# Token tiles turned by transposing DMAs instead of TensorE in an attention, FFN and MoE kernel

## The chip, the cores and the metric

The kernel runs on one core of a Trainium2 chip. The metric is the device time of one execution in microseconds (us). Engines are called PE (TensorE; PEld is its weight load), DVE (VectorE), ACT (ScalarE), POOL (GpSimd) and SP (SyncE, which only issues DMAs here).

## The reference

Three stages follow each other; the output of each is the input of the next, and all of it is float32.

```python
# attention: q, k, v are (2, 8, 768, 64); 8 global keys, window of 96
scores = np.where(keep, scale * q @ k.T + bias, -1e9)
out = softmax(scores) @ v                      # x: (1536, 512)
# gated FFN, 512 -> 1536 -> 512
xn = x / sqrt(mean(x * x) + 1e-6) * rms_g
x = (silu(xn @ w_gate) * (xn @ w_val)) @ w_out
# top-2 of 8 experts, each 512 -> 1024 -> 512
noisy = x @ w_gate2 + log1p(exp(x @ w_noise)) * noise
top2, top2_w = ...                             # softmax over the two
for e in range(8):
    for k in range(2):
        mask = top2[:, k] == e
        out[mask] += top2_w[mask, k, None] * (np.maximum(x[mask] @ w1[e], 0) @ w2[e])
```

## The kernel before

The 1,536 tokens stand in 12 tiles of 128 rows. Products that need float32 accuracy are run as three products of a high and a low part (`xTh`/`xTl`, `gh`/`gl` and `zh`/`zl` for activations, `sa` and `sb` for the two weight matrices of an expert): ACT writes the high part by a copy that rounds, and DVE or POOL subtracts it from the source for the low part.

The FFN is visited by groups of tiles and pieces of its hidden width (`VISITS`). When the last piece of a group of tiles is done (`finish`), the tiles' outputs `x` are written to the DRAM tensor `x2d` and the group is routed: `route(g)` turns each tile of 128 tokens x 512 features into 4 blocks of 128 features x 128 tokens (four 128x128 transposes `pr` on PE into PSUM, L777, then one copy `x2T` on ACT, L782), multiplies them with the gate weights (`lg`, L784), picks two experts, counts ranks (`sel`, L811 to L814) and scatters the tokens' numbers and gains into the DRAM table `metad`. There are five groups (4, 2, 2, 2 and 2 tiles). After the third, the most used expert of the first 8 tiles is read into a register (`lead`), and its first 256 rows become unit 0.

The experts run as nine units. Unit 0 and unit 1 are the early and the late 256 rows of the leading expert, units 2 to 8 the other seven experts with at most 480, 448, 424, 408, 392, 384 and 368 rows. A unit's life is: SP fetches its slots `me` from `metad` (L918), POOL gathers its token rows from `x2d` in tiles of 128 (`xg`, L939), PE turns each by four transposes (`pg`, L949), and ACT and DVE write `gh` and `gl` from PSUM (L953, L954). Then for eight pieces f of the hidden width come `up` (`pz`, L982; 12 products), ReLU (`zh` on ACT, `zl` on DVE) and `down` (12 products). Gathering and turning for a unit happen during the unit ahead of it. Weights come in as `wab` by SP, two DMAs per f.

`down` has two forms. In units 2 to 6 ("wide": L1022) the result `ac` has features on the partitions and tokens along the row, so it is copied to SBUF (`oT`, two 128xcap copies on ACT, L1049, and two on DVE, L1047), turned on PE by four transposes per tile of 128 tokens (`pb`, L1054), and only then multiplied by its gain and added to the old output rows (`y`, DVE, L1060), which POOL scatters to the output (L1065). In the other units the result comes out by tokens.

The order of instructions on each engine comes from a scheduler that simulates the program, with a few forced orders (`follow`). Every engine runs its list strictly in order, so an instruction that waits holds up all that stand behind it.

Of the kernel before, what the change touches and what calls it, by code (L numbers as in the profile page):

```python
# [19 lines left out]
P = 128  # L20
# [85 lines left out]
def fused(ctx: ExitStack, tc: tile.TileContext, q, k, v, n_global, n_local, w_gate, w_val, w_out,  # L106
# [98 lines left out]
    x2d = dr.tile([NT, DM], F32, name="x2d")  # L205
    metad = dr.tile([E * CAP, 2], I32, name="metad")
# [498 lines left out]
    def down(ci, t0, nt, f, d):  # L705
# [62 lines left out]
    def route(g):  # L768
# [3 lines left out]
        for t in range(GT):  # L772
            ti = G0[g] + t
            pt = ps.tile([P, 512], F32, name=f"pr{ti}", tag=("t", "t2", "s")[t % 3])
            p3 = pt.rearrange("p (a b) -> p a b", a=DC)
            for c in range(DC):
                nc.tensor.transpose(p3[:, c, :], x2t[ti][:, c * P:(c + 1) * P], ident)  # L777
            xt = sb.tile([P, DC, P], F32, name=f"x2T{ti}", tag="n2", bufs=N2)
            if last and t % 2:
                nc.vector.tensor_copy(xt, p3)  # L780
            else:
                nc.scalar.activation(xt, p3, AF.Copy)  # L782
# [124 lines left out]
    class Unit:  # L907
        def __init__(self, n, wkey, e, s0, cap):
# [3 lines left out]
            self.rows = G0[LEAD + 1] * P if n == 0 else NT  # L912

# [22 lines left out]
        def gather(self, s):  # L936
            m = self.tiles[s][1]
            xg = sb.tile([P, DM], F32, name=f"xg{self.n}_{s}", tag="n2", bufs=N2)
            self.last = nc.gpsimd.indirect_dma_start(  # L939
                out=xg[:m], out_offset=None, in_=x2d[:self.rows], in_offset=bass.IndirectOffsetOnAxis(ap=self.ic[:m, s:s + 1], axis=0))  # L940
            self.xg[s] = xg

        def turn(self, s, behind=None):
            m = self.tiles[s][1]
            xg = self.xg.pop(s)
            pt = ps.tile([P, 512], F32, name=f"pg{self.n}_{s}", tag="to"[s % 2])
# [5 lines left out]
            ss = slice(s * P, s * P + m)  # L952
# [10 lines left out]
        def run(self, side):  # L963
# [78 lines left out]
            if wide:  # L1042
                oT = [pools["b"].tile([P, 2, 512], F32, name=f"oT{n}_{x}", tag="raw", bufs=NRAW["b"]) for x in range(2)]
                for c in range(DC):
                    o = oT[c // 2][:, c % 2, :cap]
                    if c % 2:
                        nc.vector.tensor_copy(o, acc[c][:, :cap])  # L1047
                    else:
                        nc.scalar.activation(o, acc[c][:, :cap], AF.Copy)  # L1049
# [240 lines left out]
```

## Time and profile before

| | |
|---|---|
| median of 3 runs | 796.21 us (795.85 to 796.44) |
| profiled execution | 792.5 us, span 790.8 us, granted clock 0.991 |
| PE busy | 765.7 us (97%) |
| DVE busy | 469.0 us (59%) |
| ACT busy | 358.1 us (45%) |
| POOL busy | 308.4 us (39%) |

The span reaches from the first to the last instruction. Busy time is the time in which an engine executes something; a PE that is busy through a whole stretch sets the pace of that stretch, and other engines matter there only where they make PE wait.

### The profile page before, as it was taken

Reading aid. Unit: us, or ns where it says so; the run is one execution under the profiler, and the core shown is the slowest. Engines: PE = TensorE matmul, PEld = TensorE weight load, DVE = VectorE, ACT = ScalarE, POOL = GpSimd, SP = SyncE. Lnnn points to the kernel's source line nnn. Section 1 sums busy time; section 2 is a strip of 40 time slices with the busy share of each in tenths; the row PEclk is TensorE's granted clock in tenths of the full one; section 3 lists DMA queues with packets and bytes.
Section 4 is the critical chain, followed back from the end, with each engine's and each line's share of the span. In section 5 each row is a group of like instructions: output and inputs, shape, how many; then the busy total and the mean of one; then the engine's idle time right before and its main releaser. Section 6 shows DMA issues by size and latency. Waiting matters only on the chain. (4 is left out here: it accounts for less than half of the span.)

```text
span 790.8 us, 13766 instructions
## 1 busy us (share of the span) xinstructions
PE 765.7 (97%) x5019; PEld 692.0 (88%) x5019; DVE 469.0 (59%) x1081; ACT 358.1 (45%) x792; POOL 308.4 (39%) x343
## 2 busy tenths in 40 slices
PE   9899999999999999999999999899999999999993
PEld 6788999999788888889999888788999999999993
DVE  7988776766487888334454577433534454545542
ACT  6777566656444343123333465433343434344440
POOL 3457742331385576002431253531524343424311
PEclk9999999999999999999999999999999999999998
DMA  8654442250242430011109229953545638362011
GB/s 193 149 158 108 112 110 48 52 163 2 83 131 86 127 107 1 1 54 28 26 3 231 64 40 280 281 168 123 173 135 170 199 109 258 109 221 76 36 40 36
DMA packets 116839, 88.77 MB, mean 112 GB/s; under 512 B 49449, under 2 KB 100649, under 8 KB 116768
## 3 DMA queue, kind: packets, MB, share of 16 engines
q1 hardware_dynamic: 107920, 65.43, 30.2%
q0 software_dynamic: 7120, 19.27, 7.2%
q10 hardware_dynamic: 1728, 3.15, 1.3%
q8 instruction: 41, 0.67, 0.4%
q14 instruction: 30, 0.25, 0.1%
HBM read 75.18 MB, written 13.34 MB: 112 GB/s over the span
## 5 line engine op out<-in xcount | busy, mean ns | idle before, releaser
L982 PE MATMUL pz<-gh,sa 128*128 128x256 f32 (+7 forms) x576 | 156.8, 340 | 0.0
L982 PEld LDWEIGHTS pz<-gh,sa 128*128 128x128 f32 x576 | 104.0, 189 | 4.7
L982 PE MATMUL pz<-gl,sa 128*128 128x256 f32 (+7 forms) x288 | 97.6, 339 | 0.0
L715 PE MATMUL acc<-wo,dh 128*128 128x512 f32 x288 | 89.0, 400 | 1.0 <-ACT dh L701 1.0
L1022 PE MATMUL ac<-zh,sb 128*128 128x480 f32 (+4 forms) x320 | 86.3, 364 | 0.0
L989 ACT ACTIVATE zh<-pz 128x256 fp32r<-128x256 f32 (+7 forms) x72 | 35.1, 487 | 108.8 <-PE pz L982 106.4
L990 DVE SCALAR_TENSOR_TENSOR zl<-pz,zh 128x256 fp32r<-128x256 f32 (+7 forms) x72 | 39.8, 553 | 72.6 <-ACT zh L989 72.3
L688 PE MATMUL pz<-xTh,wg 128*128 128x256 f32 x352 | 75.0, 289 | 2.4 <-ACT wg L641 1.3
L688 PE MATMUL pz<-xTh,wv 128*128 128x256 f32 x352 | 75.3, 290 | 0.0
L670 ACT ACTIVATE sa<-wab 128x512 fp32r<-128x512 f32 x72 | 45.3, 631 | 56.6 <-PE ac L1022 39.6
L688 PEld LDWEIGHTS pz<-xTh,wg 128*128 128x128 f32 x352 | 58.9, 192 | 4.8 <-ACT wg L641 1.5
L674 DVE TENSOR_TENSOR sa<-wab,sa 128x512 fp32r<-128x512 f32 x51 | 36.4, 715 | 41.7 <-ACT sa L670 41.3
L1022 PEld LDWEIGHTS ac<-zh,sb 128*128 128x128 f32 x320 | 58.0, 188 | 3.2
L702 POOL TENSOR_TENSOR dl<-u,dh 128x256 fp32r<-128x256 f32 (+1 forms) x38 | 38.7, 1019 | 56.7 <-ACT dh L701 41.7
L715 PEld LDWEIGHTS acc<-wo,dh 128*128 128x128 f32 x288 | 51.3, 189 | 9.9 <-ACT dh L701 1.7
L688 PEld LDWEIGHTS pz<-xTh,wv 128*128 128x128 f32 x352 | 58.9, 193 | 0.3
L939 POOL DMA_INDIRECT xg<-x2d,ic x30 | 30.8, 1027 | 69.9 <-PE pg L949 63.1
L982 PEld LDWEIGHTS pz<-gl,sa 128*128 128x128 f32 x288 | 54.6, 190 | 2.4
L429 ACT ACTIVATE p<-s,mx 128x256 f32<-128x256 f32 (+1 forms) x96 | 46.2, 483 | 21.8 <-DVE mx L426 21.6
L892 POOL DMA_INDIRECT metad<-meta,si x24 | 23.8, 991 | 82.4 <-DVE si L864 76.3
L715 PE MATMUL acc<-wo,dl 128*128 128x512 f32 x144 | 53.0, 400 | 0.2 <-POOL dl L702 0.2
L1022 PE MATMUL ac<-zl,sb 128*128 128x480 f32 (+4 forms) x160 | 53.0, 358 | 0.0
(249 smaller groups left out, 1856.4 us busy)
## 6 DMA issues: line engine op xcount, KB each, us to landing
wab<-in_moe_w_dram SPq DMA_DIRECT2D x128, 256.0 KB, 5.0
rg<-in_moe_w_gate_dram SPq DMA_DIRECT2D x12, 512.0 KB, 4.1
rv<-in_moe_w_val_dram SPq DMA_DIRECT2D x12, 512.0 KB, 3.7
ro<-in_moe_w_out_dram SPq DMA_DIRECT2D x12, 512.0 KB, 3.5
vn<-in_v_dram SPq DMA_DIRECT2D x12, 256.0 KB, 4.1
out_dram<-zero SPq DMA_DIRECT2D x1, 3072.0 KB, 13.2
x2d<-x ACTq DMA_DIRECT2D x12, 256.0 KB, 5.1
kn<-in_k_dram SPq DMA_DIRECT2D x11, 256.0 KB, 3.2
```

What stands on the lines that cost most here:

```text
L429: state["e"] = nc.scalar.activation(p[:, :W], s[:, :W], AF.Exp, scale=-1.0, bias=mx[:, h:h + 1], accum_out=sm[:, h:h + 1]).ins
L670: cp = nc.scalar.activation(wp[:, 0], src, AF.Copy)
L674: (nc.gpsimd if pool else nc.vector).tensor_sub(wp[:, 1], src, wp[:, 0].bitcast(F32))
L688: mm = nc.tensor.matmul(pz, a[:, cs], x[:, tt:tt + nt, c, :], start=(n == 0), stop=(n == 3 * DC - 1))
L702: (nc.gpsimd if ci < len(CHUNKS) - 1 else nc.vector).tensor_sub(dl, u, dh.bitcast(F32))
L715: nc.tensor.matmul(acc[t], a[:, tt], w, start=(f == CHUNKS[ci][0] and n == 0), stop=(end and n == 2))
L892: st = nc.gpsimd.indirect_dma_start(out=metad, out_offset=bass.IndirectOffsetOnAxis(ap=si[:, t, kk:kk + 1], axis=0), in_=meta[:, G0[g] + t ...
L939: self.last = nc.gpsimd.indirect_dma_start(out=xg[:m], out_offset=None, in_=x2d[:self.rows], in_offset=bass.IndirectOffsetOnAxis(ap=self.i ...
L982: mm = nc.tensor.matmul(pz[:, :cap], a[:, cs], x[:, c, :cap], start=(k == 0), stop=(k == 3 * DC - 1))
L989: nc.scalar.activation(dh[:, :cap], pz[:, :cap], AF.Relu)
L990: nc.vector.scalar_tensor_tensor(dl[:, :cap], pz[:, :cap], 0.0, dh[:, :cap].bitcast(F32), op0=ALU.max, op1=ALU.subtract)
L1022: nc.tensor.matmul(acc[c][:, :cap], w[:, c * P:(c + 1) * P], a[:, :cap], start=(f == 0 and k == 0), stop=(f == FB2 - 1 and k == 2))
```

## The change

A float32 row of 512 numbers is stored as 1,024 halves of 16 bits, first the 512 low halves and then the 512 high halves. A DMA that transposes 16-bit elements turns the 128 x 1,024 matrix into 8 blocks of 128 x 128, and one ACT copy puts low and high halves together again as float32 (1,024 elements per partition).

- POOL splits each of the 12 tiles into halves (`halve`, a copy of 1,024 16-bit elements), and SP writes them to a new DRAM tensor `x2p`, beside `x2d`, which stays.
- Routing turns 10 of the 12 tiles by this DMA (`turned`); the last group's two still go by PE.
- Units 0 and 3 to 8 gather from `x2p` and turn by DMA, 24 tiles in all. Units 1 and 2 are as before.
- The five wide units copy each `ac` out of PSUM as halves, in three pieces where one was, turn 4 tiles each by DMA, 20 in all, and merge them on ACT. DVE reads the merged `pb` from SBUF.

This takes 216 of the 128x128 transposes off PE, and the ten routing copies off ACT. It adds 54 transposing DMAs and 12 writes on SP's queue, 54 merging copies on ACT, and 12 copies and 5 small memsets on POOL.

```diff
+    def turned(words, m, src, name, shape, tag, bufs):
+        nc.sync.dma_start_transpose(words[:, :, :m], src)
+        xt = sb.tile(shape, F32, name=name, tag=tag, bufs=bufs)
+        x3 = xt.rearrange("p (c q) -> p c q", c=DC) if len(shape) == 2 else xt
+        x4 = x3[:, :, :m].bitcast(U16).rearrange("p c (q t) -> p t c q", t=2)
+        nc.scalar.activation(x4, words[:, :, :m].rearrange("p (t c) q -> p t c q", t=2), AF.Copy)
+        return x3
...
+    def halve(ti, behind=None):
+        hw = split2[ti] = sb.tile([P, 2, 2 * DM], U16, name=f"hw{ti}", tag="words", bufs=2)
+        cp = nc.gpsimd.tensor_copy(hw[:, 0].rearrange("p (t n) -> p t n", t=2), x2t[ti].bitcast(U16).rearrange("p (n t) -> p t n", t=2))
...
+        nc.sync.dma_start(x2p[ti * P:(ti + 1) * P, :], hw[:, 0])
...
+            if not last:
+                hw = split2[ti]
+                xt = turned(hw[:, 1].rearrange("p (a b) -> p a b", a=2 * DC), P, hw[:, 0], f"x2T{ti}", [P, DC, P], "n2", N2)
...
+            self.halved = n == 0 or n > 2
...
+            if self.halved:
+                m2 = -(-m // 16) * 16
+                if s % 2 == 0:
+                    self.hw = sb.tile([P, 2, 2 * DC, P], U16, name=f"hg{self.n}_{s}", tag="words", bufs=2)
+                x3 = turned(self.hw[:, s % 2], m2, xg[:m2], f"xc{self.n}_{s}", [P, 512], "wc", 2)[:, :, :m]
+                nc.scalar.activation(self.gh[:, :, ss], x3, AF.Copy)
+                nc.vector.tensor_sub(self.gl[:, :, ss], x3, self.gh[:, :, ss].bitcast(F32))
+                return
...
                 for c in range(DC):
...
+                    for x in range(2):
+                        w = min(2 * P, cap - 2 * x * P)
+                        src = acc[c][:, 2 * x * P:2 * x * P + w].bitcast(U16)
...
+                        for s0, k, q in pieces:
...
+                            if c % 2:
+                                nc.vector.tensor_copy(o, i)
+                            else:
+                                nc.scalar.activation(o, i, AF.Copy)
...
-                    pt = ps.tile([P, 512], F32, name=f"pb{n}_{s}", tag="to"[s % 2])
-                    for c in range(DC):
-                        nc.tensor.transpose(pt[:m, c * P:(c + 1) * P], oT[c // 2][:, c % 2, s * P:s * P + m], ident)
+                    if s % 2 == 0:
+                        back = sb.tile([P, 2, 2 * DC, P], U16, name=f"ob{n}_{s}", tag="words", bufs=2)
+                    nc.sync.dma_start_transpose(back[:, s % 2], hs[s // 2][:, s % 2].rearrange("p t c q -> p (t c q)"))
+                    pt = sb.tile([P, 512], F32, name=f"pb{n}_{s}", tag="wc", bufs=2)
+                    nc.scalar.activation(pt[:m].bitcast(U16).rearrange("p (c q t) -> p t c q", t=2, c=DC),
+                                         back[:m, s % 2].rearrange("p (t c) q -> p t c q", t=2), AF.Copy)
```

Three places of the order show how the change stands in the engines' lists. The first is ACT at the start of unit 3, behind the copies `oT` of unit 2's result (the suffix `_3` in `sa_2_3` is the unit, the number ahead of it is f). Before:

```order
L670 ACTIVATE sb_0_3_6811<-wab_0_6374 128x512 [waits DMAHW1_49,DVE_49,PE_49]
L989 ACTIVATE zh_0_6764<-pz_0_6751 128x448 [waits PE_49]
L670 ACTIVATE sa_2_3_6826<-wab_2_6439 128x512 [waits DMAHW4_49,Pool_49]
L989 ACTIVATE zh_1_6802<-pz_1_6789 128x448 [waits DVE_49,PE_49]
L670 ACTIVATE sb_1_3_6851<-wab_1_6399 128x512 [waits DMAHW3_49,Pool_49]
L670 ACTIVATE sa_3_3_6866<-wab_3_6479 128x512 [waits DMAHW6_49,DVE_49,PE_49]
L989 ACTIVATE zh_2_6842<-pz_2_6829 128x448 [waits DVE_49,PE_49]
L670 ACTIVATE sb_2_3_6891<-wab_2_6439 128x512 [waits DMAHW5_49,Pool_49]
```

Now:

```order
L672 ACTIVATE sb_0_3_6802<-wab_0_6368 128x512 [waits DVE_49,PE_49]
L1028 ACTIVATE zh_0_6755<-pz_0_6742 128x448 [waits PE_49]
L672 ACTIVATE sa_2_3_6817<-wab_2_6433 128x512 [waits DMAHW4_49,Pool_49]
L1109 ACTIVATE pb_0_6707<-ob_0_6705 128x2x512 [waits DMAHW3_49]
L1028 ACTIVATE zh_1_6793<-pz_1_6780 128x448 [waits DVE_49,PE_49]
L672 ACTIVATE sb_1_3_6842<-wab_1_6393 128x512 [waits Pool_49]
L1109 ACTIVATE pb_1_6710<-ob_0_6705 128x2x512 [waits DMAHW4_49]
L1109 ACTIVATE pb_2_6714<-ob_2_6712 128x2x512 [waits DMAHW5_49,DVE_49]
L672 ACTIVATE sa_3_3_6857<-wab_3_6473 128x512 [waits DMAHW6_49,PE_49]
L1109 ACTIVATE pb_3_6717<-ob_2_6712 96x2x512 [waits DMAHW6_49,DVE_49]
L1028 ACTIVATE zh_2_6833<-pz_2_6820 128x448 [waits PE_49]
L672 ACTIVATE sb_2_3_6882<-wab_2_6433 128x512 [waits Pool_49]
```

The four merges `pb_0` to `pb_3` of unit 2's result stand between the splits and the ReLUs of unit 3, each waiting for its transposing DMA.

The second is ACT at the end of the FFN, where tiles 8 and 9 are routed and unit 0's rows are turned (`dh_10` and `dh_11` are the FFN's last hidden pieces, which PE needs for its last `acc` products). Before:

```order
L701 ACTIVATE dh_9_5511<-u_9_5507 128x256 [waits DVE_49]
L792 ACTIVATE ny_5425<-lg_5402 128x16 [waits PE_49]
L793 ACT_TABLE_LOAD
L793 ACTIVATE ny_5425<-ny_5425 128x16 [waits Activation_49]
L696 ACT_TABLE_LOAD [waits DVE_49]
L696 ACTIVATE u_10_5548<-pz_10_5523 128x256 [waits PE_49]
L873 ACTIVATE ed_5460<-ed_5460 128x2 [waits DVE_49]
L701 ACTIVATE dh_10_5552<-u_10_5548 128x256 [waits DVE_49]
L953 ACTIVATE gh_5134<-pg_0_5562 128x4x128 [waits PE_49]
L696 ACTIVATE u_11_5594<-pz_11_5569 128x256 [waits DVE_49,PE_49]
L701 ACTIVATE dh_11_5598<-u_11_5594 128x256 [waits DVE_49]
```

Now:

```order
L713 ACTIVATE dh_9_5502<-u_9_5498 128x256 [waits DVE_49]
L708 ACTIVATE u_10_5539<-pz_10_5514 128x256 [waits DVE_49,PE_49]
L713 ACTIVATE dh_10_5543<-u_10_5539 128x256 [waits DVE_49]
L689 ACTIVATE x2T_5403<-hw_5393 128x2x512 [waits DMAHW4_49]
L708 ACTIVATE u_11_5584<-pz_11_5559 128x256 [waits DVE_49,PE_49]
L689 ACTIVATE x2T_5410<-hw_5398 128x2x512 [waits DMAHW6_49]
L689 ACTIVATE xc_0_5555<-hg_0_5553 128x2x512 [waits DMAHW7_49]
L713 ACTIVATE dh_11_5588<-u_11_5584 128x256 [waits DVE_49]
L983 ACTIVATE gh_5127<-xc_0_5555 128x4x128 [waits Activation_49]
L689 ACTIVATE xc_1_5599<-hg_0_5553 128x2x512 [waits DMAHW0_49]
L817 ACTIVATE ny_5416<-lg_5401 128x16 [waits PE_49]
L983 ACTIVATE gh_5127<-xc_1_5599 128x4x128 [waits Activation_49]
```

The routing copies have become merges and moved behind `dh_10` and `u_11`; `dh_11` now stands behind the merge `xc_0` of unit 0's first gathered tile, and the logits' `ny` behind `dh_11`.

The third is SP at the end of unit 2's stretch, where the loads `wab` of unit 3's last weights stand. Before:

```order
L902 DMA wab_6_7029<-in_moe_w_dram 128x4x128 [waits DMAHW5_49]
L905 ISA
L905 DMA wab_6_7029<-in_moe_w_dram 128x512 [waits DMAHW6_49]
L902 ISA
L902 DMA wab_7_7076<-in_moe_w_dram 128x4x128 [waits DMAHW7_49,DVE_49,Pool_49]
L905 ISA
L905 DMA wab_7_7076<-in_moe_w_dram 128x512 [waits DMAHW0_49]
L918 ISA
L918 DMA me_7186<-metad 128x4x2 [waits DMASW2_49,DMASW3_49,DMASW1_49,DMAHW1_49,DMASW0_49,DVE_49]
```

Now:

```order
L930 DMA wab_6_7016<-in_moe_w_dram 128x512 [waits DMAHW2_49]
L1107 DMA_TRANSPOSE ob_0_6705<-oT_0_6690 128x8x128 [waits DMAHW3_49,DVE_49,Activation_49]
L1107 DMA_TRANSPOSE ob_0_6705<-oT_0_6690 128x8x128 [waits DMAHW4_49]
L1107 DMA_TRANSPOSE ob_2_6712<-oT_1_6691 128x8x128 [waits DMAHW5_49,DVE_49,Activation_49]
L1107 DMA_TRANSPOSE ob_2_6712<-oT_1_6691 128x8x128 [waits DMAHW6_49,DVE_49,Activation_49]
L927 ISA
L927 DMA wab_7_7061<-in_moe_w_dram 128x4x128 [waits DMAHW7_49,DVE_49,Pool_49]
L685 DMA_TRANSPOSE hg_0_6919<-xg_0_6797 128x8x128 [waits DMAHW3_49,DMAHW0_49,DMAHW4_49,DMASW4_49,Activation_49]
L685 DMA_TRANSPOSE hg_0_6919<-xg_1_6837 128x8x128 [waits DMAHW1_49,DMASW5_49]
L685 DMA_TRANSPOSE hg_2_7010<-xg_2_6877 128x8x128 [waits DMAHW5_49,DMAHW2_49,DMAHW6_49,DMASW6_49,Activation_49]
L685 DMA_TRANSPOSE hg_2_7010<-xg_3_6917 128x8x48 [waits DMASW7_49]
```

Eight transposing DMAs, four for unit 2's results (`ob`) and four for unit 4's gathered rows (`hg`), stand between the loads; they share two buffers (tag "words").

## Rows read from the trace of the kernel before

**Rows 1.** The page: busy us, share of the span, instructions

```profile
PE 765.7 (97%) x5019; PEld 692.0 (88%) x5019; DVE 469.0 (59%) x1081; ACT 358.1 (45%) x792; POOL 308.4 (39%) x343
```

**Rows 2.** Busy us by stage: window, length, engines, PEclk, DMA share, GB/s

```profile
348.00:430.00 82.00, 81.85 (x615) 76.72 (x614) 36.28 (x149) 27.20 (x57) 21.26 (x23) 1.00 0.26 61
...
430.00:470.00 40.00, 39.21 (x293) 35.71 (x292) 26.70 (x107) 21.89 (x43) 13.69 (x12) 1.00 0.26 83
...
549.00:590.00 41.00, 41.00 (x218) 37.57 (x217) 19.67 (x31) 15.67 (x30) 14.45 (x15) 1.00 0.52 155
```

**Rows 3.** Waits of PE over the whole span: us, times, longest

```profile
PE pg L949 <- DMA xg<-x2d,ic: 3.4, 3, 2.5
```

**Rows 4.** Groups by line of two kinds of turn on PE

```profile
L1054 PE MATMUL pb<-ident,oT x80: 269/273/275, 553.3 to 718.7; 128*128 128x128 f32 x60, 128*96 128x128 f32 x4, 128*64 128x128 f32 x4, 128*40 128x128 f32 x4
...
L949 PE MATMUL pg<-ident,xg x120: 201/272/447, 440.4 to 735.2; 128*128 128x128 f32 x96, 96*128 96x96 f32 x4, 64*128 64x64 f32 x4, 40*128 40x40 f32 x4
```

**Rows 5.** Timeline of PE where turns stand between other products

```profile
432.44 0.60 PE L777 MATMUL pr<-ident,x 128*128 128x128 f32 x4
...
433.12 0.60 PE L777 MATMUL pr<-ident,x 128*128 128x128 f32 x4
...
434.01 0.63 PE L715 MATMUL acc<-wo,dh 128*128 128x512 f32 x2
...
434.48 0.39 PE L715 MATMUL acc<-wo,dl 128*128 128x512 f32 x1
...
552.85 0.56 PE L982 MATMUL pz<-gh,sa 128*128 128x448 f32 x2
...
553.25 1.03 PE L1054 MATMUL pb<-ident,oT 128*128 128x128 f32 x8
...
554.33 0.57 PE L982 MATMUL pz<-gh,sa 128*128 128x448 f32 x2
```

**Rows 6.** Timeline of ACT, DVE and PE at the start of unit 3

```profile
548.93 1.03 ACT L1049 ACTIVATE oT<-ac 128x480 f32<-128x480 f32 x2 [1.32 <-PE ac L1022]
...
549.14 1.22 DVE L1047 COPY oT<-ac 128x480 f32<-128x480 f32 x2 [3.42 <-PE ac L1022]
...
557.77 0.63 ACT L670 ACTIVATE sa<-wab 128x512 fp32r<-128x512 f32 x1 [1.37 <-PE ac L1022]
...
563.30 0.37 PE L982 MATMUL pz<-gh,sa 128*128 128x448 f32 x1
...
565.78 1.05 PE L1022 MATMUL ac<-zh,sb 128*128 128x448 f32 x4
```

**Rows 7.** Groups of ACT and POOL by line and shape: total, mean ns

```profile
L953 ACT ACTIVATE gh<-pg 128x512 fp32r<-128x512 f32 x24 | 14.1, 591 | 5.3 <-PE pg L949 5.2
...
L953 ACT ACTIVATE gh<-pg 128x256 fp32r<-128x256 f32 x1 | 0.4, 375 | 0.0
...
L674 POOL TENSOR_TENSOR sa<-wab,sa 128x512 fp32r<-128x512 f32 x21 | 27.1, 1288 | 51.0 <-ACT sa L670 46.4 <-ACT gh L953 4.4
```

**Rows 8.** DMA issues: queue, count, KB each, median us to landing

```profile
wab<-in_moe_w_dram SPq DMA_DIRECT2D x128, 256.0 KB, 5.0
...
out_dram<-zero SPq DMA_DIRECT2D x1, 3072.0 KB, 13.2
...
kn<-in_k_dram SPq DMA_DIRECT2D x2, 128.0 KB, 2.8
...
metad<-meta,si POOLq DMA_INDIRECT x24, 7.1
```

**Rows 9.** Timeline of DVE, SP and PE between the FFN and unit 0

```profile
445.75 0.16 DVE L864 CAST si<-sl 128x4 int32<-128x4 f32 x1
...
446.34 1.20 PE L715 MATMUL acc<-wo,dh 128*128 128x512 f32 x4 [0.48 <-ACT dh L701]
...
457.44 0.38 SPq L918 DMA_DIRECT2D me<-metad  x1
...
463.30 0.16 DVE L752 CAST idf<-me 128x2 f32<-128x2 int32 x1
```

More of the change, by code (lines that the diff above doesn't have):

```diff
@@ L15 @@
 U32 = mybir.dt.uint32
+U16 = mybir.dt.uint16
 AF = mybir.ActivationFunctionType
@@ L205, in fused @@
     x2d = dr.tile([NT, DM], F32, name="x2d")
+    x2p = dr.tile([NT, 2 * DM], U16, name="x2p")
     metad = dr.tile([E * CAP, 2], I32, name="metad")
@@ L728, in down @@
                 nc.scalar.dma_start(x2d[ti * P:(ti + 1) * P, :], accs[ti])
+                if ti < G0[-1]:
+                    halve(ti)
         if t0 + nt == NT // P:
@@ L773, in route @@
             ti = G0[g] + t
-            pt = ps.tile([P, 512], F32, name=f"pr{ti}", tag=("t", "t2", "s")[t % 3])
-            p3 = pt.rearrange("p (a b) -> p a b", a=DC)
-            for c in range(DC):
[L777 to L780, printed above, removed]
-            else:
-                nc.scalar.activation(xt, p3, AF.Copy)
+            if not last:
+                hw = split2[ti]
+                xt = turned(hw[:, 1].rearrange("p (a b) -> p a b", a=2 * DC), P, hw[:, 0], f"x2T{ti}", [P, DC, P], "n2", N2)
+            else:
+                pt = ps.tile([P, 512], F32, name=f"pr{ti}", tag=("t", "t2", "s")[t % 3])
+                p3 = pt.rearrange("p (a b) -> p a b", a=DC)
+                for c in range(DC):
+                    nc.tensor.transpose(p3[:, c, :], x2t[ti][:, c * P:(c + 1) * P], ident)
+                xt = sb.tile([P, DC, P], F32, name=f"x2T{ti}", tag="n2", bufs=N2)
+                if t % 2:
+                    nc.vector.tensor_copy(xt, p3)
+                else:
+                    nc.scalar.activation(xt, p3, AF.Copy)
             for c in range(DC):
@@ L951, in turn @@
                     follow(mm.ins, behind)
-            ss = slice(s * P, s * P + m)
             nc.scalar.activation(self.gh[:, :, ss], p3, AF.Copy)
@@ L1042, in run @@
             if wide:
-                oT = [pools["b"].tile([P, 2, 512], F32, name=f"oT{n}_{x}", tag="raw", bufs=NRAW["b"]) for x in range(2)]
-                for c in range(DC):
[L1045 to L1049, printed above, removed]
+                nt = len(self.tiles)
+                hs = [pools["b"].tile([P, 2, 2, DC, P], U16, name=f"oT{n}_{x}", tag="raw", bufs=NRAW["b"]) for x in range(2)]
@@ new lines, in run @@
+                e, m = self.tiles[-1]
+                if m < P:
+                    nc.gpsimd.memset(hs[e // 2][:, e % 2].rearrange("p t c q -> p (t c) q")[:, :, m:], 0)
+                for c in range(DC):
+                    for x in range(2):
+                        w = min(2 * P, cap - 2 * x * P)
+                        src = acc[c][:, 2 * x * P:2 * x * P + w].bitcast(U16)
+                        k, q = -(-w // P), min(w, P)
+                        if w % P and k > 1:
+                            pieces = [(0, 1, P), (1, 1, w - P)]
+                        else:
+                            pieces = [(0, k, q)]
+                        for s0, k, q in pieces:
+                            o = hs[x][:, s0:s0 + k, :, c, :q].rearrange("p s t q -> p t s q")
+                            i = src[:, 2 * s0 * P:2 * s0 * P + 2 * k * q].rearrange("p (s q t) -> p t s q", t=2, q=q)
+                            if c % 2:
+                                nc.vector.tensor_copy(o, i)
+                            else:
+                                nc.scalar.activation(o, i, AF.Copy)
@@ L1168, in late @@
         route(NG - 1)
+        for t in range(GS[-1]):
+            halve(G0[-1] + t, units[1].last.ins)
         for i in range(E - 1):
```

14 lines of the change are left out of this document (11 added, 3 removed).

## The prediction

> **What bounds the kernel now.** I read the page first: PE is busy for 765.7 us, 97% of the span, ACT for 45%, POOL for 39% [rows 1]. Then the table by stage: PE executes for 81.85 of 82 us where routing starts, 39.21 of 40 us between the FFN and unit 0, and all 41 us of unit 3's stretch, while ACT has 15.67 us of work there [rows 2]. The waits of PE confirm it: the largest sum behind one releaser is 3.4 us, for gathered rows, three times in all [rows 3]. So a matmul taken away is time gained, one for one, as long as what replaces it is done before PE asks for it. Three quantities decide: what a turn costs PE, how late a turned tile arrives, and what the instructions behind it in ACT's list do meanwhile.
>
> **What is removed.** The lines of `pb` and `pg` show 272 and 273 ns each [rows 4], but they are pipelined, so I take their price from the distance between neighbours. In unit 3 two `up` products begin at 552.85 and the turns at 553.25, 0.20 us a product; without turns the next pair, one product on, would begin at 553.45. It begins at 554.33, so eight `pb` cost 0.88 us, 0.110 each. From one group of four `pr` to the next, with one `acc` between them, are 0.68 us; an `acc` takes (434.48 - 434.01) / 2 = 0.235, so four turns cost 0.445, 0.111 each [rows 5]. I use 0.11 for `pg` too, whose rows show the same 272 ns. 80 + 40 + 96 = 216 turns by 0.11 make **-23.8 us**. The ten routing copies leave ACT, which isn't the bound: nothing.
>
> **The price of a transposing DMA.** No row shows one. Two numbers are needed: L, from the issue to the landing of the first, and p, the distance at which others on SP's queue follow. L is at least 2.8 us (128 KB of plain load) and at most, for an estimate, 7.1 us (scattered small pieces, `metad`). p is at least 13.2 / 12 = 1.1 us (256 KB of the 3,072 KB fill), and at most, when none overlap, a whole landing of 256 KB, 5.0 us [rows 8]. A transpose moves the 256 KB twice through SBUF in small pieces, so I place it near the middle of each, 4.5 and 2.0.
>
> [...]
>
> **What is added in the wide units.** A merge has 1,024 elements. 512 take 0.591 us on ACT and 256 take 0.375 [rows 7], so 0.84 ns an element and 0.16 fixed: 1.02 us. 54 of them are 55 us on an ACT that has 791 - 358 = 433 free, and in a unit eight of them are 8.2 us beside 15.7 of 41. Throughput is no question; order is. The halves are copied in three pieces a column, 512, 256 and under 256 elements: about 0.59 + 0.38 + 0.3 = 1.3 us for one of 0.51. The two columns on ACT then take 2.6 us where rows show 1.03 from 548.93, DVE's about 2.9 from 549.14 where rows show 1.22 [rows 6]. The first half tile pair is complete near 551.2, when both engines have done the first piece of their second column, and SP issues four transposes.
>
> ACT's list now reads: `sa_2`, merge 0, `zh_1`, `sb_1`, merges 1 and 2, `sa_3`, merge 3, `zh_2`, `sb_2`. Two needs follow. `sa_3` (before at 557.77; PE's `up` uses it at 563.30 [rows 6]) comes behind merge 2, at 551.2 + L + 2p + 1.0; then 0.63, DVE's 0.69 and some 0.6 of semaphores: ready at 554.1 + L + 2p, wanted at 563.30 - 0.88 = 562.4. It is in time while L + 2p is under 8.3. `zh_2` and `sb_2` come behind merge 3: 551.2 + L + 3p + 1.0 + 0.54 + 0.63 + POOL's 1.29 [rows 7] + 0.4 = 555.1 + L + 3p, wanted by the `down` at 565.78 - 2 x 0.88 = 564.0. So a unit loses **L + 3p - 8.9**. At 4.5 and 2.0 that is 1.6 us; five units lose **8 us**, of which I take 6.5, since the lists of units 4 to 7 have a little more of other work between merge 3 and its next need. The lower bounds (2.8, 1.1) give nothing lost, the upper (7.1, 5.0) 13 us a unit.
>
> The gathered tiles of units 3 to 8 are turned a unit ahead. SP's eight transposes a unit take 16 us of some 38, so the loads `wab` (5.0 us to land [rows 8]) behind them stay a unit ahead: nothing, while p is under about 3.5. Units 1, 2 and 8 don't follow a wide unit.
>
> **What is added around the FFN's end.** Group 3's merges stand with unit 0's: `dh_11` is behind merge `xc_0`, which waits for POOL's split of two tiles (1,024 16-bit elements; between 1.3 and 2.6 us each, from 1.29 for 512 [rows 7]), a write and three transposes. PE's products with it begin at 446.34 and already wait 0.48 [rows 9]. I take 2 us (0 to 6). Then the ranks of tiles 8 and 9, which were multiplied before `dh_11`, move behind unit 0's first `up` and `down`, some 9 us by PE's list (an estimate). In the trace `si` is ready at 445.75, the slots are fetched at 457.44, and DVE's `idf`, at 463.30, needs them landed [rows 9]: 463.3 - 457.4 - 2 for the landing (an estimate from the 2.8 of rows 8) leaves 4 of cover for a delay of 9, and behind `idf` on DVE stand `sa_5` and `zl_4` of unit 0, which PE needs; by the order they have little to spare. I take 4 us (0 to 8). The first three routing groups put merges, each behind a write and a transpose, between ACT's `u` and `dh` while PE is full [rows 2]: 2.5 us (0 to 8). Together **+8.5**. POOL's other work has room (39%), and `y` reading SBUF costs no more than PSUM: nothing.
>
> **The sum.** -23.8 + 6.5 + 8.5 = -8.8. The profiled execution took 792.5 (span 790.8, 1.7 around it): 783.7. The median is 796.21, 3.7 above it, so **787.4**.
>
> **Rivals.** (a) *All hidden.* Transposes at plain-load speed: L = 2.8, p = 1.1, L + 3p = 6.1, under 8.9, and the moved ranks cost what DVE lets pass, 2 us. -23.8 + 2 gives 774.4. For it: ACT is idle half the time. Against: the list has waits where it had none. (b) *The merges wait.* ACT stands before the merges in list order, and PE's `down` behind it. The place is merge 3 in units 3 to 7; the price is 5 (L + 3p - 8.9). With 15.3 us left over from -23.8 + 8.5, it decides from L + 3p = 12, p = 2.5 at L = 4.5. At L = 5 and p = 3, 5.1 a unit, +25.5: 806.4. For it: strict lists, two shared buffers, an unseen DMA. Against: 8.9 us of cushion. (c) *No change to speak of*: L + 3p near 12, 796. That turns don't leave PE is excluded by the order.
>
> **Chances and range.** The forecast's own case (780 to 793) gets 0.42, (a) 0.20, both faster; (c) 0.07; (b) 0.31. A difference of 0.2%, 1.6 us, is about what can be told from none here: faster 0.62, same 0.07, slower 0.31. The range runs from (a), 773, to a little past (b), 812. The forecast's own range is 780 to 793.
>
> **What would show it.** Right: PE's busy time about 23 us lower; landings of transposes near 4.5 us, 2 apart; PE's waits behind `zh`, `zl`, `sb` or `sa` of 1 to 2 us in units 3 to 7; a wait near `idf`. All hidden: no new waits of PE. Wrong: landings of 7 us or more, merges `pb` idle before on DMA for tens of us in sum, and PE waiting at each unit's start. A PE clock below 1.00 after such gaps would add to it.

## The result, and the profile after

The changed kernel took 807.93 us (805.73 to 810.66, 4 runs) where the kernel before took 796.33 (795.85 to 796.79, 4 runs): a ratio of 1.0150, 95% interval 1.0114 to 1.0187. It is 12 us slower, on the other side from the forecast of 787.4, inside the stated range of 773 to 812, but near the end that belongs to the rival in which the merges wait.

The page of the profiled execution (span 809.0 us) shows the turns gone and the time not. The columns are those of [rows 1].

```profile
PE 756.8 (94%) x4803; PEld 677.3 (84%) x4803; DVE 477.1 (59%) x1101; ACT 417.6 (52%) x856; POOL 329.7 (41%) x360
...
PEclk9999999999999999999899799999999999999997
```

PE has 4,803 products, 216 fewer, and 8.9 us less work, where 23.8 were forecast. Part of what is left ran at a lower granted clock (0.50 of full speed in the windows 401 to 407 and 446 to 450): those are the slices below 9 in the second row. The table by stage (columns as in [rows 2]) says where:

```profile
348.00:430.00 82.00, 76.02 (x545) 71.11 (x545) 34.74 (x142) 31.19 (x53) 25.22 (x27) 0.96 0.41 85
...
430.00:470.00 40.00, 30.84 (x191) 27.00 (x189) 16.27 (x50) 16.76 (x28) 7.30 (x7) 0.87 0.62 164
...
510.00:560.00 50.00, 44.67 (x214) 37.77 (x213) 21.67 (x37) 23.62 (x41) 23.11 (x24) 0.93 0.95 251
...
645.00:685.00 40.00, 39.73 (x210) 38.33 (x209) 21.19 (x38) 26.49 (x45) 18.17 (x18) 1.00 0.92 228
```

From 348 to 430 PE now stands idle for 6.0 us of 82, where it stood 0.15; from 430 to 470 for 9.2, at a mean clock of 0.87, where it stood 0.8 at 1.00 [rows 2]. In a unit in the middle (645 to 685) it stands 0.3. The waits of PE name what ended last there (us in total, times, longest):

```profile
PE pz L700 <- DVE u L710: 6.4, 2, 5.8
...
PE lg L809 <- ACT x2T L689: 5.7, 2, 5.1
...
PE ac L1061 <- ACT sb L672: 3.1, 3, 2.6
...
PE pz L1021 <- ACT xc L689: 2.8, 1, 2.8
...
PE pz L1021 <- ACT sa L672: 2.7, 2, 1.7
...
PE acc L727 <- ACT dh L713: 2.3, 2, 1.8
...
PE pz L1021 <- DVE sa L676: 2.0, 1, 2.0
```

Comparing the beginnings of the same PE work in the two timelines gives the balance by stage; this table is worked out from them.

```
                                before    after   difference
last FFN products (dh_11, dl_11) 447.6    460.6     +13.0
first product of unit 2          500.7    527.3     +26.6
first product of unit 3          549.4    573.0     +23.7
first product of unit 7          709.1    725.7     +16.7
first product of unit 8          744.6    762.8     +18.2
end of the span                  790.8    809.0     +18.2
```

So units 3 to 6 gain 7.0 us, and 23.7 are lost ahead of them. The two profiled executions are 18.2 us apart and the medians 11.6 (the one before lies 3.8 under its median, the one after 2.7 above), so the losses of this table are up to 6.6 us larger than those of the medians. Waits and clock account for the loss, near enough: between 348 and 560 four windows (three are shown; the fourth is 470 to 510) have 25.5 us of idle PE and a clock 0.04, 0.13, 0.04 and 0.07 below full over 82, 40, 40 and 50 us, which is 13.6 us, 39.1 together, against some 4.4 and 1.6 before. The 33 us between these sums stand against 23.7 us lost and some 7 us of turns saved on the way.

**The first loss, at 400.** Tiles 6 and 7, after which the leading expert is read. The timeline from the last sum of tile 6:

```profile
390.24 0.69 DVE L737 TENSOR_TENSOR x<-x,acc 128x512 f32<-128x512 f32 x1 [0.62 <-remote]
...
391.14 2.02 POOL L750 COPY hw<-x 128x1024 uint16<-128x1024 uint16 x2 [2.16 <-issue]
...
392.70 3.68 SPq L685 DMA_TRANSPOSE hw<-hw  x1
...
399.07 1.34 ACT L689 ACTIVATE x2T<-hw 128x1024 uint16<-128x1024 uint16 x1 [7.32 <-DMA hw<-hw]
...
400.47 1.89 PE L809 MATMUL lg<-wr,x2T 128*128 128x16 f32 x8 [5.08 <-ACT x2T L689]
```

The sum is there at 390.93, POOL begins to split it 0.2 us later, and the transposing DMA is issued at 392.70. Its issue takes SP 3.68 us, and the merge starts at 399.07, 6.4 us after the issue began and 8.1 after the sum. So most of the delay is the DMA's own: the DMAs of results landed in 3.3 us (below), and what this one met was not tested. In the kernel before, the sums of the same two tiles end at 393.4 and the first copy begins at 395.76, 3.0 us after the first of them:

```profile
392.11 1.29 DVE L725 TENSOR_TENSOR x<-x,acc 128x512 f32<-128x512 f32 x2 [0.24 <-PE acc L715]
...
395.76 0.60 ACT L782 ACTIVATE x2T<-pr 128x512 f32<-128x512 f32 x1 [0.47 <-PE pr L777]
```

In the changed kernel ACT stood idle for 7.3 us with the FFN's `u` behind it, and PE waited 5.08. The register follows: the first weights of unit 0 are asked for at 422.06 instead of 414.37, its slots (`me`) at 433.49 instead of 421.61.

**The second, at 446.**

```profile
433.49 0.38 SPq L944 DMA_DIRECT2D me<-metad  x1
...
436.83 0.38 SPq L927 DMA_DIRECT2D wab<-in_moe_w_dram  x1
...
443.62 1.04 ACTq L740 DMA_DIRECT2D x2d<-x  x2
...
444.76 0.38 ACT L708 ACTIVATE u<-pz 128x256 f32<-128x256 f32 x1 [9.58 <-DMA wab<-in_moe_w_dram]
...
446.11 0.58 PE L700 MATMUL pz<-xTh,wg 128*128 128x256 f32 x1 [5.76 <-DVE u L710]
```

ACT stands idle for 9.58 us ahead of `u`, and what ended last is a weight load. The two writes of `x` to `x2d` stand ahead of `u` in ACT's list, and each waits for a semaphore that a weight load of SP's queue was given; the loads issued at 436.83 and 437.40 landed at 443.54 and 444.26. The first four loads go out 7.7 us later than before and those behind the slots 11.9 (434.07 instead of 422.18), so the writes, in the same place of the list, now meet them.

**In the units.** Start of unit 3, which answers to [rows 6]:

```profile
573.87 2.08 ACT L1102 ACTIVATE oT<-ac 128x512 uint16<-128x512 uint16 x6 [1.72 <-PE ac L1061]
...
576.05 5.67 SPq L1107 DMA_TRANSPOSE ob<-oT  x4
...
579.33 1.37 ACT L1109 ACTIVATE pb<-ob 128x1024 uint16<-128x1024 uint16 x1 [1.71 <-DMA ob<-oT]
...
585.87 2.19 SPq L685 DMA_TRANSPOSE hg<-xg  x1
...
593.57 1.34 ACT L689 ACTIVATE xc<-hg 128x1024 uint16<-128x1024 uint16 x1 [3.11 <-DMA hg<-xg]
...
595.72 0.62 ACT L672 ACTIVATE sb<-wab 128x512 fp32r<-128x512 f32 x1
...
596.39 1.39 PE L1061 MATMUL ac<-zh,sb 128*128 128x448 f32 x5 [2.62 <-ACT sb L672]
```

The four result turns leave SP in 5.67 us, and the first merge starts 3.28 us after the first issue: L = 3.3, p = 1.4. The merges of results are on time. What holds ACT is further on, at 593.57: the third *gathered* tile, for which ACT stands idle 3.11 us. Its transpose was issued at 585.87, right behind the one ahead of it, and landed 7.6 us later, while weight loads and gathers were under way; what slowed it was not tested. `sb` comes behind it and PE waits 2.62. The tiles of unit 3, which are turned a unit earlier, came later still: four issues hold SP for 13.70 us, the first tile takes 12.7 us to land, and PE's wait of 2.8 behind `xc` follows:

```profile
528.84 13.70 SPq L685 DMA_TRANSPOSE hg<-xg  x4
...
541.51 1.34 ACT L689 ACTIVATE xc<-hg 128x1024 uint16<-128x1024 uint16 x1 [7.63 <-DMA hg<-xg]
```

The list of ACT by line and form says the same over the whole span (total, mean in ns, and ACT's idle time ahead of the group); a merge of 1,024 elements takes 1.36 us. Gathered rows kept ACT waiting 23.4 us, results 3.9:

```profile
L689 ACT ACTIVATE xc<-hg 128x1024 uint16<-128x1024 uint16 x19 | 25.8, 1360 | 25.8 <-DMA hg<-xg 23.4 <-SPq L1264 2.1 <-issue 0.2
...
L1109 ACT ACTIVATE pb<-ob 128x1024 uint16<-128x1024 uint16 x15 | 19.8, 1362 | 3.9 <-DMA ob<-oT 3.9
```

### The profile page after: what moved, and what is told of

The parts are those of the page before. It is cut to its first block, busy times and chain, and to the rows that moved or that the text cites. A ratio compares the mean times of both kernels' runs of the same rounds, so it can differ in the third digit from the quotient of the medians.

```text
span 809.0 us, 13546 instructions
## 1 busy us (share of the span) xinstructions
PE 756.8 (94%) x4803; PEld 677.3 (84%) x4803; DVE 477.1 (59%) x1101; ACT 417.6 (52%) x856; POOL 329.7 (41%) x360
## 2 busy tenths in 40 slices
DMA packets 172537, 105.38 MB, mean 130 GB/s; under 512 B 103569, under 2 KB 154769, under 8 KB 172464
## 5 line engine op out<-in xcount | busy, mean ns | idle before, releaser
L1061 PE MATMUL ac<-zh,sb 128*128 128x480 f32 (+4 forms) x320 | 84.3, 359 | 3.1 <-ACT sb L672 3.1
L672 ACT ACTIVATE sa<-wab 128x512 fp32r<-128x512 f32 x72 | 44.8, 624 | 23.7 <-PE ac L1038 11.2
L1121 POOL DMA_INDIRECT out_dram<-y,me x30 | 33.1, 1103 | 55.3 <-DVE y L1116 45.7
L1038 PE MATMUL ac<-sb,zh 128*128 128x512 f32 (+1 forms) x176 | 52.7, 388 | 2.1 <-ACT zh L1028 1.1
L672 ACT ACTIVATE sb<-wab 128x512 fp32r<-128x512 f32 x72 | 45.3, 630 | 16.7 <-PE ac L1038 8.3
```

The source lines that it names most:

```text
L672: cp = nc.scalar.activation(wp[:, 0], src, AF.Copy)
L1038: mm = nc.tensor.matmul(o, a[:, s * P:s * P + m], w[:, cuts(s)[x]], start=(f == 0 and k == 0), stop=(f == FB2 - 1 and k == 2)).ins
L1061: nc.tensor.matmul(acc[c][:, :cap], w[:, c * P:(c + 1) * P], a[:, :cap], start=(f == 0 and k == 0), stop=(f == FB2 - 1 and k == 2))
L1121: st = nc.gpsimd.indirect_dma_start(out=out, out_offset=bass.IndirectOffsetOnAxis(ap=self.me[:m, s, 0:1], axis=0), in_=y[:m], in_offset=No ...
```

## The experiments

Theory A: the loss is made where a tile is turned in a hurry, in routing and unit 0; the turns far ahead in the units are a gain. Rival B: the merges inside the units cost what they save. Ratios are to the kernel before, on the same chip, with 95% intervals. The scheduler lays out every list anew after an edit, and no run kept the old order, so each ratio is the edit together with its new order. Line numbers in rows are those of each kernel.

**Routing on PE again.**

```diff
-            if not last:
+            if False:
```

> All twelve tiles are turned for routing by TensorE again (40 turns more, about 4.4 us); the tiles are still split into halves and written to x2p, and units 0 and 3 to 8 and the wide results still use transposing DMAs. Theory A (the loss is made in routing: late turned tiles hold ACT's list, the leading expert's register and with it its weights come late, and TensorE falls to its lower clock after the gaps): the last FFN products start near 450 us instead of 461, the waits of TensorE behind x2T and behind the FFN's u (5.1 and 5.8 us) are gone, and the time is 786 to 793. Rival B (the loss is made by merges inside the expert units): the time is 809 to 813, since only the 4.4 us of turns come back.

797.0 us, 1.0063 (1.0033 to 1.0093), outside both stated ranges. Rival B as the whole cause is out, since 10.9 us came back where it had 4.4; but 0.9% came back where A expected 2%. The last of the FFN's products, `dh_11`, start at 458.8, as late as in the changed kernel and against A. PE now waits 7.03 us in one place, for unit 0's turned rows, and 6.6 us in another, near 531 behind `sb`, which follows the merges of unit 3's gathered rows. The first of the two (SP's wait, the landing of the two transposes, ACT, PE, and the window with its clock):

```profile
SPq L685 <- DMA x2p<-hw: 5.5, 1, 5.5
...
DMA to landing us min/median/max: 3.3/3.3/3.3
...
444.78 1.34 ACT L689 ACTIVATE xc<-hg 128x1024 uint16<-128x1024 uint16 x1 [4.93 <-DMA hg<-xg]
...
451.81 0.58 PE L1021 MATMUL pz<-gh,sa 128*128 128x256 f32 x1 [7.03 <-ACT gh L983]
...
450.00:460.00 10.00, 8.19 (x40) 0.64 0.00 1
```

These two transposes land in 3.3 us. SP held them 5.5 us, because unit 0's turned halves go to a buffer that the write of tile 8 to `x2p` still held. Over the whole run the results landed as fast and the gathered rows didn't (medians):

```profile
hg<-xg SPq DMA_TRANSPOSE x24, 5.3
...
ob<-oT SPq DMA_TRANSPOSE x20, 3.3
```

The mean granted clock of that window is 0.64: some 7 of the 10 us at 0.50 and the rest at 1.00, by an estimate from the 0.50 that the changed kernel has between 446 and 450. The window begins with a PE that stands idle until 451.81.

**The split on DVE instead of POOL.**

```diff
-        cp = nc.gpsimd.tensor_copy(hw[:, 0]...
+        cp = (nc.gpsimd if behind is not None else nc.vector).tensor_copy(hw[:, 0]...
```

> As the changed kernel, but the split into halves of the ten routed tiles is done by DVE instead of POOL. Theory A1 (the third group's tiles are late because their split stands behind eight metad scatters on POOL, 378.7 to 389): the split of tiles 6 and 7 starts some 9 us earlier, the wait of TensorE of 5.1 us behind x2T shrinks below 1, the register of the leading expert comes 5 to 9 us earlier, and with it the 5.8 us wait near 446 shrinks; time 796 to 802. Theory A2 (the transposing DMAs are slow by themselves): no change beyond 2 us, 806 to 810.

804.27 us, 1.0117 (1.0067 to 1.0167): not told apart from the changed kernel. PE still waits 3.88 us for `x2T` of that group, and the first weights are asked for at 425.3. That POOL's list was not what made the tiles late in the changed kernel is shown by its own rows, where the split begins 0.2 us after the sum. Here, in a new order, the sums already come late, at 394.9, behind a `si` on DVE that waits 3.4 us for the first group's scatters to land.

**Results on PE again; then rows on PE again.** The first puts the old `pb` block back, the second is

```diff
-            self.halved = n == 0 or n > 2
+            self.halved = n == 0
```

> As the changed kernel, but the results of the five wide units are turned by TensorE as before (80 turns more, 8.8 us), with one copy instead of three for each column. Rival B (merges of the results hold ACT and cost more than the turns): 797 to 803, and the waits of TensorE in units 3 to 7 (5.9 us in the changed kernel) are gone. Theory A (the results' part alone is a gain, and what waits there stands behind the merges of gathered rows): 811 to 817, some of those waits stay.

> As the changed kernel, but units 3 to 8 gather from x2d and are turned by TensorE as before (22 tiles, 88 turns, 9.7 us more); unit 0 stays with the DMA. Theory A with the waits in the units put down to the merges of gathered rows: the waits in units 2 to 7 (2.8 and 5.9 us) go, 9.7 us come back: 808 to 812. Rival B (the units' merges make the whole loss): 795 to 800.

810.98 us, 1.0217 (1.0179 to 1.0256), and 810.89 us, 1.0186 (1.0135 to 1.0237). Without the results' part the kernel is slower by 0.7%, the two intervals just overlapping; without the rows' part it can't be told apart from the changed kernel (1.0150). So A's claim that both parts are worth keeping is likely for the results and open for the rows; the hit of 810.89 in A's range is in part luck, since a wait that nobody had forecast is in it. With the results on PE, waits behind `sb`, `zh` and `sa` in the units stay, so they come from the gathered rows; with the rows on PE these are gone, and PE waits 10.8 us in sum for gathered rows that land late.

**Only the far-ahead parts.** Routing and unit 0 on PE (as above), and `self.halved = n > 3`; `n > 2`; or no halves at all, the results alone:

> Routing, unit 0 and unit 3 are turned by TensorE; transposing DMAs are kept for the rows of units 4 to 8 and the results of the five wide units (152 turns off TensorE, 16.7 us; all tiles are still split and written to x2p). Theory A (the loss is made where a tile is turned in a hurry: routing, unit 0, unit 3; the far-ahead turns are a gain): the stretch up to unit 3's first product is as before within 3 us, the waits of TensorE behind xc and sb ahead of it are gone, and the time is 10 to 15 us under before: ratio 0.981 to 0.988. Rival B (the DMAs and merges of the units cost what they save): within 4 us of before.

> As the kernel of late units, but unit 3's four gathered tiles also go through the DMA (16 turns more off TensorE, 1.8 us). Theory A: its merges stand behind transposes that SP reaches only after unit 3's weight loads, so ACT holds TensorE for 3 to 7 us near unit 2's first down product, as it did with routing alone undone (6.6 us): 2 to 7 us slower than the kernel of late units. Rival B: 1 to 2 us faster than it.

> Only the results of the five wide units go through transposing DMAs (80 turns off TensorE, 8.8 us); routing and all gathered rows are turned by TensorE, nothing is split and x2p is not written. Theory A with the waits of units 3 to 7 put down to the merges of gathered rows: no waits behind sa, sb or zh in units 3 to 7, 7 to 10 us under before: ratio 0.987 to 0.991. Rival B (the results' merges make those waits, 5.9 us): 2 to 4 us under before.

788.18 us, 0.9908 (0.9880 to 0.9935); 786.72 us, **0.9890 (0.9860 to 0.9920)**; 798.96 us, 1.0039 (1.0013 to 1.0065). The first falls a little short of what A expected. The second beats the kernel before and the changed one. It is not told apart from the first, so the DMA for unit 3's tiles costs nothing on balance, as Rival B had it, although PE waits 4.9 us for them in unit 2 as A said. Its page and one window:

```profile
PE 753.0 (96%) x4851; PEld 676.8 (86%) x4851; DVE 476.1 (61%) x1101; ACT 408.2 (52%) x854; POOL 331.3 (42%) x360
...
645.00:685.00 40.00, 40.00 (x219) 1.00 1.03 278
```

Results alone are 0.4% *slower* than before, against both theories. The results arrive later than on PE: POOL's scatters begin 8.2 us after unit 3's first product where they began 5.8 us after it, and the gathers stand behind them in POOL's list (POOL's timeline, and PE's wait over the span):

```profile
561.48 1.05 POOL L1119 DMA_INDIRECT out_dram<-y,me  x1 [3.03 <-DVE y L1114]
...
581.84 0.90 POOL L967 DMA_INDIRECT xg<-x2d,ic  x1 [0.31 <-issue]
...
PE pg L987 <- DMA xg<-x2d,ic: 9.9, 4, 3.3
```

A PE that turns gathered rows at a fixed place of its list waits for them. Before, the same gathers were the ones that waited, for PE to free a buffer.

**Rows alone**, the fourth corner (results, routing, unit 0 on PE):

> The fourth corner beside results only (ratio 1.004) and both (0.989): the gathered rows of units 3 to 8 through the DMA (88 turns off TensorE, 9.7 us), results, routing and unit 0 on TensorE. Theory A5 (results alone lose because they make POOL's scatters and so the next gathers late, which a TensorE that turns gathered rows in a fixed place must wait for; rows alone have no such chain): 6 to 10 us under before, ratio 0.987 to 0.993, waits of TensorE only around unit 3's start. Rival (the gain needs both): ratio 0.998 to 1.004.

798.33 us, 1.0037 (1.0010 to 1.0064): the gain needs both halves, the rival's case. PE waits 3.9 and 2.8 us in unit 2 and 0.3 to 1.5 behind `sb`, `zh` or `sa` in the units after it. Why ACT is later there than with both is not settled.

**The `x2d` write off ACT.** The changed kernel with the writes of tiles 8 and 9 issued by SP:

```diff
-                nc.scalar.dma_start(x2d[...], accs[ti])
+                (nc.sync if G0[3] <= ti < G0[4] else nc.scalar).dma_start(x2d[...], accs[ti])
```

> As the changed kernel, but the writes of tiles 8 and 9 to x2d are issued by SP, behind the weight loads, instead of ACT. Theory A3 (the write on ACT waits for a completion slot that a late weight load holds, and holds the FFN's u for 9.6 us behind it): ACT's wait ahead of u near 444 shrinks from 9.6 us to 2 or 3 (what remains is the wait for the FFN's own products), TensorE's wait of 5.8 us near 446 goes, and the clock near 440 to 460 stays nearer 1.0: 6 to 10 us under the changed kernel, 798 to 802. Rival (u waits for something else, such as the weights themselves): no change beyond 2 us.

804.89 us, 1.0103 (1.0069 to 1.0137). PE's wait of 5.8 us behind `u` is gone, so the write was what held ACT. The time is not told apart from the changed kernel's 1.0150: the writes and transposes of tiles 8 and 9 now stand behind the loads on SP, and PE waits for them instead.

```profile
442.65 1.63 SPq L740 DMA_DIRECT2D x2d<-x  x2
...
445.68 1.47 SPq L685 DMA_TRANSPOSE hw<-hw  x1
...
452.88 3.59 PE L809 MATMUL lg<-wr,x2T 128*128 128x16 f32 x16 [8.34 <-ACT x2T L689]
```

**Unit 0 with buffers of its own**, routing on PE:

```diff
+                ww = self.hw[:, s % 2] if self.n else sb.tile([P, 2 * DC, P], U16, ..., tag="acc", bufs=NACC)
```

> Routing on TensorE and unit 0's two tiles through the DMA, as in the kernel with routing undone (797.0 us, ratio 1.006), but unit 0's turned halves are given two buffers of their own instead of the pair that the writes of tiles 8 and 9 to x2p still hold. Theory A4 (the transposes wait 5.5 us for those writes to land, through the shared buffers, and ACT's merge holds the FFN's u, the second half of gh and with them TensorE for 7.0 us): SP's wait behind x2p is gone, the 7.0 us wait of TensorE is under 2, the clock stays near 1.0 from 440 to 460, and the time is 785 to 789, ratio 0.986 to 0.992, level with TensorE turning unit 0. Rival (the gathered rows themselves land too late, or the merges are in the way wherever they stand): ratio 1.002 to 1.008, as with the shared buffers.

794.21 us, 0.9981 (0.9953 to 1.0009): about half of unit 0's price (from 1.0063) came back; 0.989 was not reached. SP no longer waits for `x2p`, but the order put the merge ahead of the FFN's `u`, and there it waited 12.26 us for rows gathered in the middle of unit 0's weight loads (SP, ACT, PE):

```profile
432.33 4.68 SPq L685 DMA_TRANSPOSE hg<-xg  x2
...
438.10 1.34 ACT L689 ACTIVATE xc<-hg 128x1024 uint16<-128x1024 uint16 x1 [12.26 <-DMA hg<-xg]
...
440.77 1.97 PE L802 MATMUL pr<-ident,x 128*128 128x128 f32 x8 [8.17 <-DVE x L737]
```

**Unit 0 on PE, routing by DMA**, and then that with the routing merges on POOL:

```diff
-            self.halved = n == 0 or n > 2
+            self.halved = n > 2
...
+        if tag == "n2":
+            nc.gpsimd.tensor_copy(x4, w4)
```

> As the changed kernel, but unit 0's two tiles are gathered from x2d and turned by TensorE; routing stays with the DMA. If the prices of routing (0.9% in the comparison with unit 0 by DMA) and of unit 0 (1.7% with routing by TensorE) add: 1.015 - 0.017 = 0.998 of before, and TensorE waits still for x2T (4 to 5 us near 400) and for u near 446. If they overlap (both hold the same place of ACT's list), unit 0 alone gives back little: 1.008 to 1.014.

> As the kernel with unit 0 on TensorE (ratio 1.013; only routing, the rows of units 3 to 8 and the results by DMA), but the routing merges are done by POOL instead of ACT, so ACT's u and dh stand behind no late tile. Theory A6 (the price of routing by DMA is that ACT's list waits for the turned tile and holds the FFN behind it): TensorE's waits behind ACT and DVE between 390 and 470 shrink below 3 us in sum, ratio 0.995 to 1.004. Rival (the price is the lateness itself: the turned tile, and with it the leading expert's register, weights and rows come some 8 to 12 us later, whoever merges; TensorE waits for those instead): the weights of unit 0 are still asked for after 420, and the ratio stays 1.008 to 1.016.

807.65 us, 1.0133 (1.0095 to 1.0171), and 818.69 us, 1.0322 (1.0279 to 1.0366). The prices overlap: unit 0 by DMA costs 1.7% with routing on PE and 0.2%, not told apart from nothing, with routing by DMA; routing by DMA costs 2.4% with unit 0 on PE and 0.9% with unit 0 by DMA. The merges on POOL are worse still, outside what either side expected. ACT is free, but POOL's list, with the scatters that carry the slots, now waits for the turned tiles, and the first weights are asked for at about 436. So it isn't ACT alone that must not wait.

**One routing group at a time**, on top of the fastest kernel:

```diff
-            if not last:
+            if g == 0:        # then 2, then 3
```

> The fastest kernel so far (rows of units 3 to 8 and results by DMA, routing and unit 0 on TensorE, ratio 0.989) with the first routing group alone (tiles 0 to 3) turned by DMA. Theory A7 (the price of routing by DMA is the lateness of the turns on the way to the leading expert's register and to unit 0): the first group is far ahead of both, ratio 0.986 to 0.992. Rival (each late merge costs alike wherever it stands, ten of them 2.4%): four tiles cost 1.0%, ratio 0.996 to 1.002.

> As the fastest kernel, with the third routing group alone (tiles 6 and 7, after which the leading expert is read) turned by DMA. Theory A7: the first weight load of unit 0 comes at 418 to 423 instead of 414.8, the slots of unit 0 3 to 8 us later, and this group makes half of the price or more: ratio 1.000 to 1.010. Rival (all alike): two tiles, 0.5%: 0.992 to 0.996.

> As the fastest kernel, with the fourth routing group alone (tiles 8 and 9, between the last FFN products and unit 0) turned by DMA. Theory A7: the ranks and with them unit 1's slots come 5 to 9 us later, and the last FFN products wait for ACT: ratio 0.994 to 1.004. Rival (all alike): 0.992 to 0.996; or nothing, 0.989, if only the register counts.

806.03 us, 1.0113 (1.0050 to 1.0176); 792.48 us, 0.9948 (0.9912 to 0.9983); 802.40 us, 1.0056 (1.0022 to 1.0091). Against 0.9890 that is 2.2%, 0.6% and 1.7%. Theory A7 falls for the first group, which stands ahead of the register's and costs most, and for the third: there the first weights are asked for at 422.5 instead of 414.8 and the slots 5.9 us later, as A7 said, and it costs only 0.6%. So late weights are not the main price. The rival of like prices (1.0, 0.5, 0.5) holds for the third group alone. For the fourth, unit 1's slots come 6.8 us later, as A7 said, but the last FFN products are not late. Group 0's timeline on POOL and PE shows how lateness travels:

```profile
355.42 1.04 POOL L750 COPY hw<-x 128x1024 uint16<-128x1024 uint16 x1 [5.91 <-ACT x2T L689]
...
379.19 1.26 POOL L917 DMA_INDIRECT metad<-meta,si  x1 [8.57 <-DVE si L889]
...
395.07 0.97 POOL L917 DMA_INDIRECT metad<-meta,si  x1 [5.59 <-DVE si L889]
...
420.07 0.24 POOL L956 TENSOR_SCALAR ic<-me 128x2 int32<-128x2 int32 x1 [7.50 <-DMA me<-metad]
...
423.27 0.74 POOL L714 TENSOR_TENSOR dl<-u,dh 128x256 fp32r<-128x256 f32 x1
...
424.06 0.80 PE L727 MATMUL acc<-wo,dl 128*128 128x512 f32 x1 [6.50 <-POOL dl L714]
```

Its four tiles go through two shared buffers, so the third split waits 5.91 us for a merge. Its eight scatters begin at 379.19, where the kernel before had them at 370.64, the next group's at 395.07 (388.05), the fetch of unit 0's slots is not back when POOL's list reaches `ic`, and the FFN's `dl`, which needed nothing of all this, is done at 424: PE waits 6.50 us for it. The first weights are asked for at 407.6, earlier than the 414.37 of the kernel before, so the new order has its part in this as well. More buffers for routed tiles were not tried.

## Why the prediction was wrong

- **Turns off PE, -23.8**: right in kind and, where nothing else was in the way, in size. (The rows have 273 ns for `pb` and 272 for `pg`, not the other way round, which changes nothing.) In units 3 to 6, 124 turns go, 13.6 us by 0.11, and the waits there are 4.1: 9.5, where the table has 7.0; the other 2.5 are not explained.
- **The price of a transposing DMA (L 4.5, p 2.0)**: too high for results, 3.3 us from issue to landing and 1.4 apart on SP. With these L + 3p - 8.9 is below zero: the merges of results cost nothing, as rival (a) had it. For gathered and routed tiles it was too low. With routing on PE the medians were 3.3 for results and 5.3 for gathered tiles; in the changed kernel single gathered tiles took up to 12.7 us and single routed ones up to 6.4, so the prediction's own sign, landings of 7 us or more, came in part true. The 3.3 and 5.3 us stand beside 5.0 for plain 256 KB loads [rows 8]. The pieces are small, as the prediction had it: the changed kernel moves 54,120 more packets of under 512 B than the one before (103,569 instead of 49,449), about 1,000 for each of the 54 transposing DMAs. HBM reads are 75.2 MB in both, so the pieces went from SBUF to SBUF. SP spent 1.27 to 1.47 us on an issue (medians of the three kinds), and results followed each other at that distance.
- **Merges of results, +6.5**: the size came out (5.85 us of waits in units 3 to 7) for another reason, which is luck. "The gathered tiles of units 3 to 8 are turned a unit ahead... nothing" was a wrong step: their merges stand in ACT's list as well, and it stood idle 25.8 us in all ahead of them (23.4 for the DMA), most of it unnoticed by PE. That cover was checked for SP's loads and not for ACT's list.
- **Merge 1.02 us**: 1.36, a third more. The six pieces of a result took 2.08 us on ACT where 2.6 were forecast, and a split 1.04 where 1.3 to 2.6 were.
- **`dh_11`, 2 us**: 1.84. **`idf`, 4 us**: 2.0 behind `sa`, and 0.6.
- **The step that failed is the third of that part: "The first three routing groups put merges... 2.5 us (0 to 8). Together +8.5."** At unit 3's first product 23.7 us were lost in the profiled executions (somewhat less in the medians), with 7 us of turns saved on the way, and that stretch holds routing, unit 0 and unit 3's gathered tiles. A turn in routing was priced as a pause of ACT. The trace shows a chain of split, write, transpose and landing: from the sum to the merge of the first tile of groups 0 to 2 it took 6.6, 7.4 and 8.1 us, and 9.5 to 16.0 for the tiles behind it, which go through two shared buffers, where PE had 3.0 to 4.2 before (7.7 for a fourth tile). Behind it, in lists that were laid out for earlier arrivals, came ranks, scatters, the register, the loads, and FFN work (`u`, `dh`, `dl`) that has nothing to do with routing. PE waited 5.08 us near 400 and 5.76 near 446, and after these gaps its granted clock was 0.50 for some microseconds (401 to 407 and 446 to 450). The prediction named the lower clock as a sign and gave it no price; by the windows it made some 12 us.
- **Rival (b)** forecast 806.4 with the place and the mechanism wrong: not merge 3 in units 3 to 7, and not from p. The range's upper end, 812, comes from it, so that 807.93 lies inside the range is luck.

What stays open: how the loss divides between the groups (singly they cost 2.2, 0.6 and 1.7%, all together 2.4), how much of each is the scheduler's new order, what slows the landing of gathered and routed tiles, and why the rows alone gain nothing.

## What to carry to other kernels

A transfer that replaces an engine's work must be costed from the moment its input exists to the moment the first consumer may start, and then set against the place where that consumer stands in its engine's list; where the engine's turn came microseconds after its input, the DMA chain came late here, and everything behind the consumer with it, related or not. The same turn was a gain a whole unit ahead, for rows and results together. Take such a change apart by distance to its consumer before taking it whole: here the far half was 1.1% faster and the whole 1.5% slower.

## What the runs showed of the hardware

- A transposing DMA of 128 x 1,024 16-bit elements took SP 1.27 to 1.47 us to issue (medians; up to 4.6 in the changed kernel). From issue to landing it took 3.3 us for results (median of 20) and 5.3 for gathered rows (median of 24; routing on PE), up to 12.7 in the changed kernel.
- ACT, POOL, DVE: a merging copy of 1,024 16-bit elements with interleaved halves took 1.36 us on ACT; the split of as many took 1.04 us on POOL. `y` took DVE 0.75 us whether it read `pb` from SBUF (752 ns, mean of 15) or, in the kernel before, from PSUM (748 ns).
- Two DMA writes in ACT's list kept its arithmetic idle for 9.58 us: each waited for a semaphore that a weight load of SP's queue held until it landed, 6.7 and 6.9 us after its issue.
- PE's products stood 0.21 us apart instead of 0.12 for some 5 us after a gap of 7.03 us (routing on PE), in a window with a mean granted clock of 0.64 (450 to 460). In the changed kernel the granted clock was 0.50 from 446 to 450, behind a gap of 5.76 us.
